# Attention's drain and the first blocks of two dense layers, recorded as one region: five weight conversions, two in-blocks and the PSUM pools put in other places

## The chip, the cores and the metric

The kernel runs on one core of a Trainium2 chip. The metric is the device time of one launch in microseconds (us). The time before is the median of three runs. Times inside the kernel come from one profiled execution, whose clock starts with the span. TensorE is PE in the rows, its weight loads PEld; VectorE is DVE, ScalarE ACT, GpSimd POOL, SyncE SP.

## The reference

Sliding-window attention with a few sink keys feeds two dense layers, one after the other; nothing but the last result is written out.

```python
# q, k, v: (2, 8, 768, 64) fp32; n_sink = 4, window = 128
keep = is_sink | ((rel >= 0) & (rel < window))
a = softmax(where(keep, q @ k.T / 8, -1e9))
x = (a @ v) as (1536, 512)              # tokens x model width
h = np.maximum(x @ w_in1, 0.0)          # w_in: (512, 2048)
x = h * h @ w_out1                      # w_out: (2048, 512)
h = x @ w_in2                           # the second layer
g = h * np.tanh(log1p(exp(h)))
out = g @ w_out2                        # (1536, 512) fp32
```

The weights come in fp64 and are read as pairs of 32-bit words; q, k and v are fp32. A product in the layers must be as exact as fp32, so each operand is held as a high and a low part (names in h and l: `xh`, `xl`, `wih`, `wil`, `woh`, `wol`, `gh`, `gl`), and each product is three matmuls, low times high, high times low, high times high.

## The kernel before, in words

**Attention.** The work is cut into 48 pairs of heads: two batches, six tiles of 128 tokens, four pairs a tile. One loop, with `n` from -3 to 52, runs all of it as a pipeline: in step n the scores of pair n+4 are made (`emit_s`, L398), the exponentials of pair n+3 (L419), the sums' reciprocals (L430, L431) and POOL's normalisation of two pairs (L439), the transposes of two pairs (L451), their copies out of PSUM (`pts`, L466) and the products with v of pairs n-4 and n-3 (L488). When the four pairs of a tile are through, ACT copies the result out of PSUM (`xf`, L503), POOL makes its high part (L504) and its low part (L506); for the last two tiles DVE makes the low part instead, two steps later (`split_x`, L513). From n = 44 on no new scores are made: this is the **drain**. It lies between some 75 and 90 us of the span.

**Layers.** The hidden width of 2048 is cut into 16 blocks of 128, the tokens into three groups of 512. For one group and one block there is an **in-block** (12 matmuls at L195, x with `wi`, into one PSUM bank `h`) and an **out-block** (12 matmuls at L658, g with `wo`, added up over the 16 blocks in four banks `o`). Between them, for layer one, ACT does relu, square and the cast to the high part `gh` (L204, L205, L206) and DVE the low part `gl` (L209). `slot(n)` emits in-block n and, one block behind in layer one (`LAG`), the out-block.

**Conversions.** The weights of a block, `wi` and `wo`, are converted in the first pass, each by one `Conv`: SP loads 512 KB of raw words (three buffers, so a load waits until the third one before it has been read), `head` on ACT (L128) or POOL (L130) scales the high words, DVE clears all but their sign (`mid_r1`, L136), writes 16 bits of the low words (`mid_r2`, L142, the 16-bit step) and joins both (`mid_or`, L148, the or-step); `high` is a cast on ACT (L167) and `low` a subtraction on DVE (L171). The heads and the or-step's operands stand in five buffers. In the layers a planner gives two conversions to each slot, in the order of `needed` and without those in `done_w`. Inside attention they are placed by hand: `PLAN` says in which step n which stages of which block run, the block numbers 0 to 3 being wi0, wo0, wi1, wo1. `PLAN` holds three of them, wi0, wo0 and wi1; in-blocks 0 and 1 are emitted in the steps `IN_AT`, so that the planner starts at the first out-block and in-block 2.

**Order.** Both parts are recorded under `tc.manual_schedule()`, attention in one region and the layers in a second: what is written first is issued first on its engine. Attention's PSUM holds four banks for scores and early in-blocks (`ps_s`), three for transposes (`ps_p`) and one for results (`ps_a`), in this order. The layers' pools take the same eight banks: `ps_h` the first four, `ps_o` the last four. A bank is handed on when its last reader is done.

Of the kernel before, what the change touches and what calls it, by code (L numbers as in the profile page):

```python
# [9 lines left out]
F32 = mybir.dt.float32  # L10
# [6 lines left out]
PSUM = bass.MemoryType.PSUM  # L17
P = 128
# [5 lines left out]
def f32(ap):  # L24
    return ap.bitcast(F32)
# [3 lines left out]
def kernel(  # L29
# [17 lines left out]
    NB = S // P  # L47
    NPAIR = H // 2
    NDC = DM // P
    TS = 512  # L50
# [133 lines left out]
    conv = main.enter_context(tc.tile_pool(name="conv", bufs=2))  # L184
    W1N = 2
    EV = (0, 2)
    w1pool = main.enter_context(tc.tile_pool(name="w1pool", bufs=1))
    gpool = main.enter_context(tc.tile_pool(name="gpool", bufs=1, reuse_waits="tile"))
    wt = {}


    def in_products(ph, w, sp):
        for m, (a, x) in enumerate([("wil", xh[sp]), ("wih", xl[sp]), ("wih", xh[sp])]):
            for d in range(NDC):
                nc.tensor.matmul(  # L195
                    ph, lhsT=w[a][:, d, :], rhs=x[:, d, :],
                    start=(m == 0 and d == 0), stop=(m == 2 and d == NDC - 1),
                )

    def new_g(pool):  # L200
        return [pool.tile([P, TS], F32R, tag=nm, name=nm, bufs=2) for nm in ("gh", "gl")]

    def relu_squared(ph, gh):
        nc.scalar.activation(out=ph, in_=ph, func=AF.Relu)  # L204
        nc.scalar.activation(out=ph, in_=ph, func=AF.Square)  # L205
        nc.scalar.copy(gh, ph)  # L206

    def low_part(x, gh, gl):
        nc.vector.tensor_tensor(out=gl, in0=x, in1=f32(gh), op=ALU.subtract)  # L209


    att = ExitStack()
    apool = att.enter_context(tc.tile_pool(name="apool", bufs=1))
    ps_s = att.enter_context(tc.tile_pool(name="ps_s", bufs=4, space=PSUM, reuse_waits="tile"))
    ps_p = att.enter_context(tc.tile_pool(name="ps_p", bufs=3, space=PSUM, reuse_waits="tile"))
    ps_a = att.enter_context(tc.tile_pool(name="ps_a", bufs=1, space=PSUM, reuse_waits="tile"))

    tiles = [(b, i) for b in range(B) for i in range(NB)]
    qn, kn, vn = {}, {}, {}
# [280 lines left out]
    def emit_x(b, i):  # L500
        hi, lo = x_slot(b, i)
        x = apool.tile([P, NPAIR, P], F32, tag="xf", name="xf", bufs=1)
        nc.scalar.copy(x, av.pop((b, i)))  # L503
        nc.gpsimd.tensor_copy(hi, x)  # L504
        if b * NB + i < len(tiles) - 2:
            nc.gpsimd.tensor_tensor(out=lo, in0=x, in1=f32(hi), op=ALU.subtract)  # L506
        else:
            st["x"] = (x, hi, lo)
# [4 lines left out]
            nc.vector.tensor_tensor(out=lo, in0=x, in1=f32(hi), op=ALU.subtract)  # L513

    blocks = []
    for fb in range(W1N):
        wt[0, fb] = weight_tiles(w1pool, fb)
        blocks += [Conv(conv, 0, fb, part, wt[0, fb]) for part in ("wi", "wo")]
    WARM = (6, 3, 2, 1)
    PLAN = {  # L520
        0: {5: "load", 11: "head", 14: "mid_r1", 18: "mid_r2", 22: "mid_or", 26: "high low"},
        2: {36: "load", 41: "head_pool", 44: "mid_r", 45: "mid_or", 46: "high low"},
        1: {37: "load", 46: "head mid_r", 47: "mid_or", 48: "high low"},
    }

    IN_AT = (46, 48)
    SINKS = {n0 + 2 * (i - 2): i for n0 in (-1, NB * NPAIR - 3) for i in range(2, NB)}
    early, ready = {}, {}
    NPR = len(pairs)
    with tc.manual_schedule():  # L530
        load_limits()
        nc.scalar.preload_act_table_set("natural_log_exp_and_others")
        load_tile(0, "qk", halves=2)
        load_tile(1, "qk")
        load_tile(2, "kq")
        load_tile(0, "v")
        load_tile(3, "kq")
        positions()
        load_tile(1, "v")
        load_tile(2, "v")  # L540
        load_rest(2)
        warm = apool.tile([P, P], F32, name="warm")
        nc.vector.memset(warm, 0.0)
        nc.vector.memset(one, 1.0)
        nc.gpsimd.memset(two, 2.0)
        for x in prs:
            nc.gpsimd.memset(x[:, :, WIN:], 0.0)
        for x in sums:
            nc.vector.memset(x, 1e-9)
        idle = ps_a.tile([P, P + 2], F32, tag="av", name="idle")  # L550

        def keep_warm(times):
            for _ in range(times):
                nc.tensor.matmul(idle[:, 0:P], lhsT=warm, rhs=warm, start=True, stop=True)  # L554

        keep_warm(WARM[0])
        limits(idle[:, P : P + 2])
        first_mask()
        prep(0, "q", 0)
        keep_warm(WARM[1])  # L560
        prep(0, "k", 0)
        keep_warm(WARM[2])
        emit_s(*pairs[0])
        emit_max(*pairs[0], 0)
        emit_max(*pairs[0], 1)
        prep(0, "q", 1)
        prep(0, "k", 1)
        emit_s(*pairs[1])
        emit_max(*pairs[1], 0)
        emit_max(*pairs[1], 1)  # L570
        second_mask()
        window_masks()
        emit_exp(*pairs[0])
        for n in range(-3, NPR + 5):
            at = {d: pairs[n + d] for d in range(-4, 5) if 0 <= n + d < NPR}
            last = {d for d in at if at[d][2] == NPAIR - 1}
            t, j = divmod(n, NPAIR)
            if n % 2 and 0 in at:
                emit_t([at[-1], at[0]])
            if 4 in at and n > -3:  # L580
                emit_s(*at[4])
            if 3 in at and n > -3:
                emit_exp(*at[3])
            if 4 in at and n > -3:
                emit_max(*at[4], 0)
            if 4 in at and n > -3:
                emit_max(*at[4], 1)
            if n % 2 == 0:
                split_x()
                group = [at[d] for d in (2, 3) if d in at]  # L590
                if group:
                    emit_rs(group)
                for p in group:
                    emit_norm(*p)
            if -4 in last:
                emit_x(*at[-4][:2])

            if n % 2 == 0:
                if n >= 0 and j == 2:
                    prep_rows(t + 2)  # L600
                for d in (-4, -3):
                    if d in at:
                        emit_av(*at[d])
            for _ in range((1, 2, 0, 1)[j]):
                evac_t()
            if n in (-3, -2):
                prep(1, "qk"[n + 3])
            if n >= 0 and j == NPAIR - 1:
                load_tile(t + 4, "q", halves=1 + (t + 5 == len(tiles)))
                load_tile(t + 4, "k", halves=1 + (t + 6 >= len(tiles)))  # L610
                load_tile(t + 3, "v")
                load_rest(t + 3)
            if n in SINKS:
                sink_keys(SINKS[n])
            if n < 0:
                keep_warm(WARM[3])
            if n == 1:
                fast_flag()
            for fb in range(W1N):
                if n == IN_AT[fb]:  # L620
                    early[fb] = ps_s.tile([P, TS], F32, tag="s", name="h")
                    in_products(early[fb], wt[0, fb], 0)
                if n == IN_AT[fb] + 1:
                    ready[fb] = new_g(gpool)
                    relu_squared(early[fb], ready[fb][0])
                if n == IN_AT[fb] + 2:
                    low_part(early[fb], *ready[fb])
            for m, steps in PLAN.items():
                for step in steps.get(n, "").split():
                    getattr(blocks[m], step)()  # L630
    att.close()


# [259 lines left out]
    w2pool = mo.enter_context(tc.tile_pool(name="w2pool", bufs=1, reuse_waits="tile"))  # L893
    ps_h = mo.enter_context(tc.tile_pool(name="ps_h", bufs=4, space=PSUM, reuse_waits="tile"))
    ps_o = mo.enter_context(tc.tile_pool(name="ps_o", bufs=4, space=PSUM, reuse_waits="tile"))
    engines = [getattr(mybir.EngineType, e) for e in ("PE", "DVE", "Activation", "Pool", "SP")]
    tc.mark_branch_hint_location("general", hint="LikelyTaken", engines=engines)
    with tc.manual_schedule():
        moe(
            wt, lambda fb: w1pool if fb < W1N else w2pool, conv, gpool, ps_h, ps_o,  # L900
            done_in=ready, done_w=[(0, blocks[m].fb, blocks[m].part) for m in PLAN],
        )
    mo.close()
    main.close()

# [97 lines left out]
    with tc.If(is_fast == 0, label="general"):  # L1003
        dense_attention()
        gm = ExitStack()
        conv = gm.enter_context(tc.tile_pool(name="conv2", bufs=2))
        wpool = gm.enter_context(tc.tile_pool(name="wpool2", bufs=1))
        tmp = gm.enter_context(tc.tile_pool(name="tmp2", bufs=1))
        ps_h = gm.enter_context(tc.tile_pool(name="ps_h2", bufs=4, space=PSUM))
        ps_o = gm.enter_context(tc.tile_pool(name="ps_o2", bufs=4, space=PSUM))  # L1010
# [36 lines left out]
```

## Time and profile before

| what | value |
|---|---|
| median of 3 runs | 614.74 us (614.39 to 615.74) |
| the profiled execution | 614.09 us |
| its span | 612.3 us |
| PE busy | 602.5 us, 98% of the span |
| PEld busy | 493.7 us, 81% |
| DVE busy | 452.9 us, 74% |
| ACT busy | 349.6 us, 57% |
| POOL busy | 70.6 us, 12% |

The span is what lies between the first and the last instruction; the execution's own time is 1.8 us longer. Busy shares are means over the whole span, and the kernel has two parts with different limits, so they say little on the place that the change touches. In the profile's picture of 40 equal slices (15.3 us each) PE stands at nine tenths or more in all but two, the sixth (76.5 to 91.8 us) and the last.

### The profile page before, as it was taken

How to read it: one execution, taken by the hardware profiler on the slowest of the kernel's cores; microseconds unless marked ns; L12 is line 12 of the kernel's file. 1: busy time of each engine (PE TensorE's matmuls, PEld its weight loads, DVE VectorE, ACT ScalarE, POOL GpSimd, SP SyncE). 2: the span in 40 equal slices, each digit the busy share in tenths (PEclk: the TensorE clock that was granted, in tenths of full speed). 3: DMA queues.
4: the chain of work that ended last, by engine and by line, in shares of the span. 5: the costliest groups of instructions: out<-in, count | busy, mean ns of one | idle time of the engine just before them, and what ended most of it. 6: DMA issues, size and time to landing. Idle time of an engine off the chain costs nothing.

```text
span 612.3 us, 10256 instructions
## 1 busy us (share of the span) xinstructions
PE 602.5 (98%) x3854; PEld 493.7 (81%) x3854; DVE 452.9 (74%) x951; ACT 349.6 (57%) x723; POOL 70.6 (12%) x103
## 2 busy tenths in 40 slices
PE   9999989999999999999999999999999999999996
PEld 6786778888888888888888888888888888888885
DVE  5898889989621111188889699999888778887784
ACT  4999976777643333277777555555454444544442
POOL 5889940000000000000000000000000000000000
PEclk9999999999999999999999999999999999999999
DMA  9989746666400000036666300000010000100001
GB/s 190 191 179 185 195 139 179 202 204 196 148 1 0 2 0 1 0 113 197 205 190 193 101 1 2 0 1 1 1 69 1 0 1 0 44 27 1 0 1 71
DMA packets 71704, 49.45 MB, mean 81 GB/s; under 512 B 49508, under 2 KB 66148, under 8 KB 71652
## 3 DMA queue, kind: packets, MB, share of 16 engines
q1 hardware_dynamic: 71360, 48.38, 29.1%
q8 instruction: 31, 0.51, 0.3%
q10 hardware_dynamic: 292, 0.39, 0.2%
q14 instruction: 21, 0.17, 0.1%
HBM read 45.61 MB, written 3.15 MB: 80 GB/s over the span
## 4 chain that ended last, share of the span: by engine, by line
PE 94%; DVE 2%; POOL 1%; ACT 1%; issue 1%; DVEq 0%; ACTq 0%; POOLq 0%
PE o L658 43%; PE h L195 42%; PE s L398 3%; PE av L488 3%; PE pt L451 2%; PE idle L554 1%; PE tr L346 1%; POOL pr L439 1%; DVE cv_r L142 0%; PE tr L328 0%; ACT pr L419 0%; DVE cv_a L148 0%; DVE pts L466 0%; DVE s L409 0%; DVE cv_r L136 0%
## 5 line engine op out<-in xcount | busy, mean ns | idle before, releaser
L195 PE MATMUL h<-xh,wil 128*128 128x512 f32 x384 | 102.9, 390 | 0.0
L195 PE MATMUL h<-xl,wih 128*128 128x512 f32 x384 | 102.6, 389 | 0.0
L195 PE MATMUL h<-xh,wih 128*128 128x512 f32 x384 | 102.6, 389 | 0.0
L209 DVE TENSOR_TENSOR gl<-h,gh 128x512 fp32r<-128x512 f32 x48 | 33.2, 691 | 89.7 <-ACT gh L206 89.7
L195 PEld LDWEIGHTS h<-xl,wih 128*128 128x128 f32 x384 | 72.1, 188 | 15.0
L195 PEld LDWEIGHTS h<-xh,wih 128*128 128x128 f32 x384 | 72.1, 188 | 15.0
L195 PEld LDWEIGHTS h<-xh,wil 128*128 128x128 f32 x384 | 71.9, 188 | 15.0
L658 PE MATMUL o<-gh,wol 128*128 128x512 f32 x192 | 74.8, 390 | 1.5 <-DVE wol L171 1.5
L726 ACT ACTIVATE e<-t,small 128x512 f32<-128x512 f32 x48 | 34.8, 725 | 70.4 <-DVE t L722 70.4
L658 PE MATMUL o<-gh,woh 128*128 128x512 f32 x192 | 74.7, 389 | 0.0
L658 PE MATMUL o<-gl,woh 128*128 128x512 f32 x192 | 74.7, 389 | 0.0
L204 ACT ACTIVATE h<-h 128x512 f32<-128x512 f32 x48 | 27.9, 582 | 77.9 <-PE h L195 77.9
L658 PE MATMUL o<-wol,gh 128*128 128x512 f32 x176 | 68.5, 389 | 0.0
L658 PE MATMUL o<-woh,gl 128*128 128x512 f32 x176 | 68.5, 389 | 0.0
L658 PE MATMUL o<-woh,gh 128*128 128x512 f32 x176 | 68.5, 389 | 0.0
L742 ACT CAST gh<-t 128x512 fp32r<-128x512 f32 x44 | 27.4, 623 | 46.4 <-PE o L658 43.0
L148 DVE SCALAR_TENSOR_TENSOR cv_a<-cv_a,cv_r 128x512 int32<-128x512 int32 x64 | 44.6, 697 | 6.2
L209 DVE TENSOR_TENSOR gl<-t,gh 128x512 fp32r<-128x512 f32 x44 | 30.3, 689 | 19.8 <-ACT gh L742 19.8
L419 ACT ACTIVATE pr<-s,nm 128x208 f32<-128x208 f32 (+2 forms) x96 | 40.5, 436 | 5.3 <-DVE nm L409 4.9
L439 POOL TENSOR_TENSOR pr<-pr,rs 128x416 f32<-128x416 f32 (+2 forms) x48 | 42.3, 902 | 9.5 <-DVE rs L431 6.3
L658 PEld LDWEIGHTS o<-gh,wol 128*128 128x128 f32 x192 | 36.0, 188 | 8.9 <-DVE wol L171 1.6
L128 ACT ACTIVATE cv_a<-raw 128x512 f32<-128x512 f32 x63 | 42.3, 673 | 0.2 <-DMA raw<-in_moe_w_in_dram 0.2
(107 smaller groups left out, 998.1 us busy)
## 6 DMA issues: line engine op xcount, KB each, us to landing
raw<-in_moe_w_in_dram SPq DMA_DIRECT2D x32, 512.0 KB, 4.0
raw<-in_moe_w_out_dram SPq DMA_DIRECT2D x32, 512.0 KB, 4.3
vn<-in_v_dram SPq DMA_DIRECT2D x12, 256.0 KB, 5.7
qn<-in_q_dram SPq DMA_DIRECT2D x10, 256.0 KB, 5.0
kn<-in_k_dram SPq DMA_DIRECT2D x9, 256.0 KB, 4.6
vx<-in_v_dram SPq DMA_DIRECT2D x16, 128.0 KB, 4.1
out_dram<-ob SPq DMA_DIRECT2D x8, 256.0 KB, 2.4
kn<-in_k_dram SPq DMA_DIRECT2D x6, 128.0 KB, 3.0
```

What stands on the lines that cost most here:

```text
L128: nc.scalar.activation(out=self.a, in_=high_words, func=AF.Copy, scale=2.0**-112)
L148: nc.vector.scalar_tensor_tensor(out=ai, in0=ai, scalar=3, in1=self.r, op0=ALU.logical_shift_left, op1=ALU.bitwise_or)
L195: nc.tensor.matmul(ph, lhsT=w[a][:, d, :], rhs=x[:, d, :], start=(m == 0 and d == 0), stop=(m == 2 and d == NDC - 1),)
L204: nc.scalar.activation(out=ph, in_=ph, func=AF.Relu)
L209: nc.vector.tensor_tensor(out=gl, in0=x, in1=f32(gh), op=ALU.subtract)
L398: nc.tensor.matmul(banks[e][qs, 0:w], lhsT=kt[r, j, q1], rhs=kt[r, j, k0 : k0 + w], start=True, stop=True, skip_group_check=True,)
L419: nc.scalar.activation(out=pr[b, i][:, 2 * j + e, 0:w], in_=banks[e][:, 0:w], func=AF.Exp, bias=nm[:, e : e + 1], scale=-1.0, accum_out=sm ...
L439: nc.gpsimd.tensor_tensor(out=x, in0=x, in1=rs.to_broadcast([P, 2, w]), op=ALU.mult)
L488: nc.tensor.matmul(av[b, i][e * D : (e + 1) * D, j, qs], lhsT=x[0:kv, 2 * j + e, :], rhs=pts[0:kv, c, e, qs], start=(j == 0 and m == 0), s ...
L658: nc.tensor.matmul(acc[sp][t], lhsT=a, rhs=x, start=(fb == 0 and m == 0), stop=(fb == NFB - 1 and m == 2),)
L726: nc.scalar.activation(out=e, in_=t, func=AF.Ln, bias=two)
L742: nc.scalar.copy(g_tiles(n)[0], et[n][1])
```

## The change

The two regions become one. The PSUM pool `ps_a` is made first, ahead of `ps_s` and `ps_p`. `PLAN` gets two more conversions, numbers 4 (wi2) and 3 (wo1), and the others' steps move; the head of number 2 (wi1) goes from POOL to ACT. In-blocks 0 and 1 are emitted in steps 44 and 49 instead of 46 and 48, and ahead of the step's other work; their relu, square and cast follow at the end of the same step, their low parts in steps 45 and 51. Of the last two attention tiles only the last but one has its low part on DVE. The weights of block 2 get buffers in the first pool, because they are now converted inside attention.

```diff
@@ PSUM pools
+    ps_a = att.enter_context(tc.tile_pool(name="ps_a", bufs=1, space=PSUM, reuse_waits="tile"))
     ps_s = att.enter_context(tc.tile_pool(name="ps_s", bufs=4, space=PSUM, reuse_waits="tile"))
     ps_p = att.enter_context(tc.tile_pool(name="ps_p", bufs=3, space=PSUM, reuse_waits="tile"))
-    ps_a = att.enter_context(tc.tile_pool(name="ps_a", bufs=1, space=PSUM, reuse_waits="tile"))
@@ emit_x
-        if b * NB + i < len(tiles) - 2:
+        if b * NB + i != len(tiles) - 2:
             nc.gpsimd.tensor_tensor(out=lo, in0=x, in1=f32(hi), op=ALU.subtract)
@@ blocks, PLAN
-    for fb in range(W1N):
+    for fb in range(W1N + 1):
...
-        2: {36: "load", 41: "head_pool", 44: "mid_r", 45: "mid_or", 46: "high low"},
-        1: {37: "load", 46: "head mid_r", 47: "mid_or", 48: "high low"},
+        2: {36: "load", 44: "head mid_r mid_or", 45: "high", 46: "low"},
+        1: {37: "load", 45: "head mid_r1", 46: "mid_r2 mid_or", 47: "high", 48: "low"},
+        4: {38: "load", 48: "head mid_r1", 49: "mid_r2 mid_or high", 50: "low"},
+        3: {46: "load", 50: "head mid_r", 51: "mid_or", 52: "high low"},
...
-    IN_AT = (46, 48)
+    IN_AT, LOW_AT = (44, 49), (45, 51)
...
-    with tc.manual_schedule():
+    order = ExitStack()
+    order.enter_context(tc.manual_schedule())
+    if True:
@@ the loop over n: at its start
+            for fb in range(W1N):
+                if n == IN_AT[fb]:
+                    early[fb] = ps_s.tile([P, TS], F32, tag="s", name="h")
+                    in_products(early[fb], wt[0, fb], 0)
@@ the loop over n: at its end
-            for fb in range(W1N):
-                if n == IN_AT[fb]:
-                    early[fb] = ps_s.tile([P, TS], F32, tag="s", name="h")
-                    in_products(early[fb], wt[0, fb], 0)
-                if n == IN_AT[fb] + 1:
-                    ready[fb] = new_g(gpool)
-                    relu_squared(early[fb], ready[fb][0])
-                if n == IN_AT[fb] + 2:
-                    low_part(early[fb], *ready[fb])
             for m, steps in PLAN.items():
                 for step in steps.get(n, "").split():
                     getattr(blocks[m], step)()
+            for fb in range(W1N):
+                if n == IN_AT[fb]:
+                    ready[fb] = new_g(gpool)
+                    relu_squared(early[fb], ready[fb][0])
+                if n == LOW_AT[fb]:
+                    low_part(early[fb], *ready[fb])
     att.close()
@@ the layers
-    with tc.manual_schedule():
-        moe(
-            wt, lambda fb: w1pool if fb < W1N else w2pool, conv, gpool, ps_h, ps_o,
-            done_in=ready, done_w=[(0, blocks[m].fb, blocks[m].part) for m in PLAN],
-        )
+    moe(
+        wt, lambda fb: w1pool if fb <= W1N else w2pool, conv, gpool, ps_h, ps_o,
+        done_in=ready, done_w=[(0, blocks[m].fb, blocks[m].part) for m in PLAN],
+    )
+    order.close()
```

What this does to the built order is seen at three places. The first is PE's queue at the beginning of the drain, just behind the last scores; `h` is in-block 0, `av` are the products with v of pairs 40 and 41.

```order
 L451 MATMUL pt<-ident,pr_108 128x64 x16
 L398 MATMUL s<-kt 64x208 x4
+L195 MATMUL h<-xh_67,wil_111 128x512 x4
+L195 MATMUL h<-xl_70,wih_110 128x512 x4
+L195 MATMUL h<-xh_67,wih_110 128x512 x4
 L488 MATMUL av<-pts,vn 64x64 x2
 L488 MATMUL av<-pts,vx 64x64 x4
```

In-block 0 stands ahead of these products now; it stood behind them, before the next transposes.

The second place is ACT's queue where in-block 1 is turned into g: numbers at the end of a name are buffers, `h_2041` and `gh_2056` before and `h_2055` and `gh_2071` now are in-block 1, and the digit behind `wih` or `woh` is the weight block. Before:

```order
L167 CAST woh0_112<-cv_a_1987 128x512
L204 ACTIVATE h_2041<-h_2041 128x512
L205 ACTIVATE h_2041<-h_2041 128x512
L206 CAST gh_2056<-h_2041 128x512
L503 COPY xf_2078<-av_2022 128x512
L167 CAST wih2_2121<-cv_a_2109 128x512
L128 ACTIVATE cv_a_2131<-raw_2107 128x512
L167 CAST woh1_116<-cv_a_2115 128x512
```

Now:

```order
L167 CAST woh0_112<-cv_a_1981 128x512
L128 ACTIVATE cv_a_2051<-raw_1740 128x512
L167 CAST wih2_118<-cv_a_2051 128x512
L204 ACTIVATE h_2055<-h_2055 128x512
L205 ACTIVATE h_2055<-h_2055 128x512
L206 CAST gh_2071<-h_2055 128x512
L128 ACTIVATE cv_a_2093<-raw_2005 128x512
L503 COPY xf_2098<-av_2032 128x512
L167 CAST woh1_116<-cv_a_2093 128x512
```

The head and the cast of wi2 stand ahead of in-block 1's three steps; the cast reads what DVE's or-step on `cv_a_2051` leaves.

The third place is DVE's queue ahead of the low part of in-block 2, the last row of both pieces. Before:

```order
L171 TENSOR_TENSOR wol1_117<-cv_a_2115,woh1_116 128x512
L136 TENSOR_SCALAR cv_r_2140<-raw_2127 128x512
L142 TENSOR_SCALAR cv_r_2140<-raw_2127 128x512
L148 SCALAR_TENSOR_TENSOR cv_a_2139<-cv_a_2139,cv_r_2140 128x512
L171 TENSOR_TENSOR wil3_2162<-cv_a_2131,wih3_2161 128x512
L136 TENSOR_SCALAR cv_r_2172<-raw_2129 128x512
L142 TENSOR_SCALAR cv_r_2172<-raw_2129 128x512
L148 SCALAR_TENSOR_TENSOR cv_a_2171<-cv_a_2171,cv_r_2172 128x512
L171 TENSOR_TENSOR wol2_2124<-cv_a_2139,woh2_2123 128x512
L209 TENSOR_TENSOR gl_2189<-h_2175,gh_2188 128x512
```

Now:

```order
L171 TENSOR_TENSOR wol2_121<-cv_a_2136,woh2_120 128x512
L136 TENSOR_SCALAR cv_r_2161<-raw_2148 128x512
L142 TENSOR_SCALAR cv_r_2161<-raw_2148 128x512
L148 SCALAR_TENSOR_TENSOR cv_a_2160<-cv_a_2160,cv_r_2161 128x512
L171 TENSOR_TENSOR wil4_2183<-cv_a_2152,wih4_2182 128x512
L136 TENSOR_SCALAR cv_r_2193<-raw_2150 128x512
L142 TENSOR_SCALAR cv_r_2193<-raw_2150 128x512
L148 SCALAR_TENSOR_TENSOR cv_a_2192<-cv_a_2192,cv_r_2193 128x512
L171 TENSOR_TENSOR wol3_2145<-cv_a_2160,woh3_2144 128x512
L209 TENSOR_TENSOR gl_2210<-h_2196,gh_2209 128x512
```

The same in-block's low part stands behind the conversions of wo2, wi4 and wo3 where it stood behind those of wo1, wi3 and wo2: each slot of the layers works two conversions further ahead.

## Rows read from the trace of the kernel before

**Rows 1.** Stretches of the span (us): busy time of each engine.

```profile
core 0: us, PE busy (x) PEld busy (x) DVE busy (x) ACT busy (x) POOL busy (x), PEclk, DMA share, GB/s
80.00:100.00 20.00, 18.42 (x147) 14.84 (x147) 18.73 (x35) 15.04 (x27) 3.91 (x5) 1.00 0.58 180
...
130.00:140.00 10.00, 10.00 (x45) 8.26 (x45) 8.91 (x18) 7.23 (x13) 0.00 (x0) 1.00 0.63 186
```

**Rows 2.** The chain in order of time, 77 to 97 us: start, length, what.

```profile
77.82 0.17 DVE rs L430
...
79.14 1.42 DVE cv_r L142
...
81.84 0.63 ACT wih L167
...
89.58 0.61 DVE wol L171
...
90.24 3.02 PE o L658 x12
93.26 2.72 PE h L195 x12
```

**Rows 3.** Timeline of PE: start, length, instruction, [idle before, who ended it].

```profile
76.43 0.34 PE L488 MATMUL av<-pts,vn 128*64 128x64 f32 x4 [0.34 <-ACT xf L503]
...
78.31 0.46 PE L451 MATMUL pt<-ident,pr 64*128 64x64 f32 x8 [0.33 <-POOL pr L439]
...
90.24 0.50 PE L658 MATMUL o<-gh,wol 128*128 128x512 f32 x1 [1.47 <-DVE wol L171]
...
101.48 0.39 PE L658 MATMUL o<-gl,woh 128*128 128x512 f32 x1
```

**Rows 4.** Timeline of DVE, 78 to 100 us.

```profile
78.68 0.42 DVE L136 TENSOR_SCALAR cv_r<-raw 128x512 int32<-128x512 int32 x1
...
81.04 0.76 DVE L148 SCALAR_TENSOR_TENSOR cv_a<-cv_a,cv_r 128x512 int32<-128x512 int32 x1
...
96.42 0.42 DVE L136 TENSOR_SCALAR cv_r<-raw 128x512 int32<-128x512 int32 x1
96.87 0.47 DVE L142 TENSOR_SCALAR cv_r<-raw 128x512 uint16<-128x512 uint32 x1
97.44 0.69 DVE L148 SCALAR_TENSOR_TENSOR cv_a<-cv_a,cv_r 128x512 int32<-128x512 int32 x1
98.05 0.68 DVE L171 TENSOR_TENSOR wol<-cv_a,woh 128x512 fp32r<-128x512 f32 x1
98.65 0.68 DVE L209 TENSOR_TENSOR gl<-h,gh 128x512 fp32r<-128x512 f32 x1
```

**Rows 5.** Timeline of ACT, 87 to 92 us.

```profile
87.72 0.58 ACT L204 ACTIVATE h<-h 128x512 f32<-128x512 f32 x1 [0.33 <-PE h L195]
88.33 0.58 ACT L205 ACTIVATE h<-h 128x512 f32<-128x512 f32 x1
88.95 0.59 ACT L206 CAST gh<-h 128x512 fp32r<-128x512 f32 x1
89.43 0.59 ACT L503 COPY xf<-av 128x512 f32<-128x512 f32 x1
89.91 0.63 ACT L167 CAST wih<-cv_a 128x512 fp32r<-128x512 f32 x1
90.43 0.69 ACT L128 ACTIVATE cv_a<-raw 128x512 f32<-128x512 f32 x1
```

**Rows 6.** Timeline of POOL, 74 to 80 us.

```profile
75.04 1.53 POOL L130 TENSOR_SCALAR cv_a<-raw 128x512 f32<-128x512 f32 x1
```

**Rows 7.** The page's DMA issues: KB each, median us from issue to landing.

```profile
raw<-in_moe_w_out_dram SPq DMA_DIRECT2D x32, 512.0 KB, 4.3
```

**Rows 8.** Stretches at the end of the span; the last matmul ends in the first.

```profile
607.00:608.00 1.00, 0.34 (x2) 0.00 (x0) 0.61 (x2) 0.37 (x1) 0.00 (x0) 1.00 0.99 377
...
610.00:611.00 1.00, 0.00 (x0) 0.00 (x0) 0.00 (x0) 0.00 (x0) 0.00 (x0) 0.74 0.03 8
611.00:612.00 1.00, 0.00 (x0) 0.00 (x0) 0.00 (x0) 0.00 (x0) 0.00 (x0) 0.50 0.00 0
```

## The prediction, made before the changed kernel ran

> **What bounds the kernel now.** I read four views in this order: stretches, the chain that ended last, then the timelines of PE, DVE and ACT over the place that the edit touches. Read the stretches [rows 1] for one thing: inside the layers PE is busy for all of every stretch (10.00 of 10 us), while the stretch from 80 to 100 us leaves PE 1.58 us idle. Once the layers run dense, PE alone sets the pace, and whatever PE loses in attention's drain or in the first blocks is carried to the end unchanged. So the question is only when PE gets through the first blocks.
>
> The chain in time [rows 2] says what holds that place. From 77.82 us to 90.24 us the chain runs almost wholly over DVE (one ACT cast between), and it ends in the wol part of block 0, which the first out-block's first matmul needs. PE's own timeline agrees [rows 3]: it waits 0.34 us for the xf copy, 0.33 us for POOL's normalisation, and 1.47 us for that wol, 2.14 us in all. Later, at 101.48, PE reads the gl of in-block 2 with no wait; DVE began that gl at 98.65 and took 0.68 [rows 4], so it was ready about 2.1 us early. Those 2.1 us are the only slack in the place. DVE is the bound of the drain, not PE and not ACT.
>
> **What the change does on each engine.** PE: in-block 0 moves ahead of the attention products of pairs 40 and 41. No matmul is added; PE is filled where it waited 0.34 and 0.33 us, so both can go: a gain of at most 0.67 us there, and PE reaches the first out-block at 90.24 - 1.47 - 0.67 = 88.10 us. POOL: it loses the head of block 2, 1.53 us [rows 6], and gets the low part of the last attention tile (it belongs to the third group of tokens, first read two groups of 16 blocks of 2 x 2.72 us later [rows 2], 174 us, so its place is free). ACT: gets that head, 0.69 us [rows 5], some 4 us ahead of the first ACT step that the chain holds (81.84) [rows 2]; cost 0. SP: one load of 512 KB moves ahead of where it stood, the others keep their order; loads are priced below.
>
> DVE: here is the term that decides. The planner in the layers is told that five conversions are done, so its slots 0, 1 and 2 now hold the next ones: wi3, wo2, wi4, wo3 and the first half of wi5, where wi2, wo1, wi3, wo2 and half of wi4 stood. In-block 2 is the same block in both kernels, and its gl stands behind all of them. DVE therefore does two whole conversions more before that gl. One conversion is four instructions, whose starts are 0.45, 0.57, 0.61 and 0.60 us apart (96.42, 96.87, 97.44, 98.05, 98.65) [rows 4]: 2.22 us. Two are 4.44 us, against 2.1 us of slack, and DVE was the bound before it: there is no idle DVE time in front into which they could go.
>
> **The sum, step by step.** DVE starts the first conversion of the drain at 78.68 in both. Its first three instructions and one pts copy are the same four instructions in another order; before, they take until 81.65 (81.04 plus 0.61) [rows 4]. I take 81.65 for the change too. Uncontended they would take 0.45 + 0.57 + 0.60 + 0.60 = 2.22 us instead of 2.97; the 0.75 us between is the 16-bit step, which took 1.42 us there [rows 2] and 0.47 at 96.87. POOL was busy beside it before, and its normalisation of the last pairs, 1.5 us earlier without the head, is still beside it now. The Trainium skill, GPSIMD Engine Reference, section Key points, says that GpSimd shares its SBUF interfaces with VectorE and contends with two-port and two-input instructions. By that rule the 1.42 us stays, by a free POOL the sum would be 0.75 us smaller.
>
> Then eleven DVE instructions follow back to back: the first mask step of wo0 0.45, gl 0, wil1 0.60 each, wo0's 16-bit step 0.57 and its or-step 0.60, xl, pts and wol0 0.60 each, and wi2's three, 0.45, 0.57, and 0.69 to its end: 87.98 us. ACT now casts wih2 only after that (88.03; 0.05 us is the hand-over, as 90.24 after 89.58 + 0.61 shows within a few hundredths). Behind the cast wait, on ACT, the three steps of in-block 1 and the head of wo1. Their starts are 0.52, 0.61, 0.62 and 0.48 us apart and the head takes 0.69 [rows 5]: ACT ends the head at 90.95. DVE meanwhile does wil2 (from 88.70, behind the cast's 0.62) and two steps of wo1, and waits at its or-step until 91.00. That step 0.60 and gl 1 0.69: 92.29 us.
>
> In the built program the first matmul of out-block 0 waits for this gl 1. Its accumulator takes the bank that in-block 1 held, since the pools now stand in another order; before, it took a bank of the transposes. PE goes on at 92.33, against 90.24: **2.09 us lost**, with 4.2 us idle.
>
> The second wait: the or-step of wo1 releases ACT's cast of woh1, and DVE takes wol1 at 92.40, 0.60 us. Then five half conversions of 1.62, four low parts of 0.60 and gl 2, 0.69: 8.10 + 2.40 + 0.69 from 93.00 gives 104.19. PE reads it at 104.24. PE alone would be there at 92.33 + 4 blocks of 2.72 + 0.23 = 103.44. So **0.80 us more**, and against 101.48 in all **2.76 us**. Every later slot holds 5.04 us of DVE work (two conversions and a gl) against PE's 5.44, so nothing is lost further on, and nothing is won back.
>
> Loads: raw takes 4.3 us from issue to landing [rows 7]. The load of wo3 is issued after the 16-bit step of wi3, at 94.0, lands at 98.3, and DVE reads it first at 99.06 (after three half conversions and two low parts): it fits, by 0.8 us. Cost taken 0; at the other end, a load 1.3 us later than the row says lets DVE's chain slip by 0.5 us.
>
> The profiled execution took 614.09 us; the sum gives 616.85. The median of the runs shown is 0.65 us above the profiled one, so the forecast for the median is 614.74 + 2.76 = **617.5 us**. About 0.2% (1.2 us) is what a measurement of this kernel can tell from no change.
>
> **The rivals.** First, **no change**: DVE runs the same list without one wait and without contention. From 78.68 the 41 instructions up to gl 2 then take 23.07 us (mine: 25.51, with 0.75 for POOL and 1.69 of three waits for ACT, 0.81, 0.67 and 0.21). That ends at 101.75, and PE is 0.32 us late: 615.1 us. It is the floor of the DVE work. For it: POOL does end earlier. Against it: the cast of wih2 stands ahead of in-block 1's steps on ACT's queue, which makes two of these waits certain. It decides if these costs are under about 0.9 us instead of 2.44. Chance 0.10.
>
> Second, **faster**: the drain's 2.14 us of PE waits [rows 3] go and no new one comes: 612.6 us. That needs gl 2 by 99.3, so DVE's list in 20.6 us, which is under the floor of 23.07. It could only come from DVE steps that run quicker than any row shows. Chance 0.04.
>
> Third, **the clock**. After the last matmul PE is idle, and the granted clock of 1.00 (the upper level, 2.4 GHz) is 0.74 between 610 and 611 and then 0.50, the lower level [rows 8], some 3 us after it stopped. The new idle stretch is 4.2 us. The Trainium skill, TensorE: Matmul & The Clock Gate, section Why this matters for your kernels, says that an idle stretch of about this kind between bursts puts the clock back, and it speaks against this change. If out-block 0 runs at half, it takes 2.72 us more; 0.80 of that passes inside the second wait, so 1.92 remains: 619.4 us. For it: the row. Against it: no row shows a fall between two bursts. How long it would stay is not shown either; from 0 to both of the next blocks (another 2.72 us) is possible. Chance 0.17.
>
> **How the numbers follow.** My forecast has 0.69, with its own bounds from 616.7 (POOL contends with nothing, less 0.75) to 618.0 (loads, plus 0.5). The range 615.8 to 619.0 holds that, the lower half of the clock's case (0.09) and the upper edge of the first rival (0.03). Faster 0.04; within 0.2% 0.09, from the first rival; slower 0.87.
>
> **What would show it.** Right: PE idle of some 4 us before the first out-block, released by DVE's gl at L209 and not by wol; a second PE wait near 104 us for gl; DVE busy without larger gaps from 78 to 104; the waits of 0.34 and 0.33 us gone; the layers after 110 us all PE. Wrong: the first out-block starts before 90.2 us, or gl 2 ends before 102 us. If the granted clock falls under 1.00 around 92 us, the third rival holds.

## The result, and the profile after

The changed kernel takes **619.66 us** (median of 6 runs, 618.88 to 620.74), the kernel before 615.04 (6 runs in the same sessions, 614.39 to 616.09): a ratio of 1.0075, with a 95% interval of 1.006 to 1.009. It is slower by 4.6 us. The forecast was 617.5 and its range ended at 619.0: the sign was right, the size was not.

The profiled execution took 619.09 us, its span is 617.3. Four of its views answer to the rows of before. The first is the chain in order of time; its last reduce of attention's sums (L430) is the mark from which places are counted below, because the profiled executions come to it at different times (77.11 to 78.53 us).

```profile
77.34 0.17 DVE rs L430
...
88.53 0.62 ACT wih L167
...
92.15 0.61 DVE gl L209
...
92.81 4.94 PE o L663 x12
97.75 2.74 PE h L195 x12
```

Before, the chain's last DVE step ahead of the first out-block was wol [rows 2]; now it is gl at L209, the low part of in-block 1. The out-block behind it takes 4.94 us there, where 12 matmuls took 3.02 before. PE's timeline says when it waited.

```profile
82.00 0.71 PE L451 MATMUL pt<-ident,pr 64*128 64x64 f32 x15 [0.41 <-DVE pts L466]
83.13 0.34 PE L488 MATMUL av<-pts,vn 128*64 128x64 f32 x4 [0.42 <-ACT xf L503]
...
88.03 0.29 PE L488 MATMUL av<-pts,vn 128*64 128x64 f32 x4
92.81 0.79 PE L663 MATMUL o<-gh,wol 128*128 128x512 f32 x1 [4.49 <-DVE gl L209]
...
105.77 0.39 PE L663 MATMUL o<-gh,wol 128*128 128x512 f32 x1
106.00 0.40 PE L663 MATMUL o<-gl,woh 128*128 128x512 f32 x1
```

The waits of 0.34, 0.33 and 1.47 us [rows 3] are gone; 0.41, 0.42 and 4.49 stand in their place. Out-block 2 starts at 105.77. From the mark that is 28.43 us, and 23.43 before (its second matmul at 101.48 [rows 3], its first at 101.25): 5.00 us later. PE reads gl 2 at 106.00 without a wait. The stretches show the granted clock, in the last column but two.

```profile
85.00:90.00 5.00, 3.31 (x42) 2.52 (x40) 4.18 (x9) 2.62 (x5) 0.00 (x0) 1.00 0.60 178
90.00:91.00 1.00, 0.00 (x0) 0.00 (x0) 0.67 (x2) 0.97 (x3) 0.00 (x0) 0.56 0.40 160
91.00:92.00 1.00, 0.00 (x0) 0.00 (x0) 0.54 (x1) 0.90 (x2) 0.04 (x1) 0.50 0.00 0
...
96.00:97.00 1.00, 1.00 (x4) 0.81 (x3) 0.97 (x3) 0.80 (x2) 0.00 (x0) 0.52 0.47 90
97.00:98.00 1.00, 1.00 (x6) 0.82 (x5) 0.90 (x3) 0.58 (x2) 0.00 (x0) 1.00 0.97 377
...
110.00:120.00 10.00, 10.00 (x46) 8.29 (x45) 9.45 (x19) 7.72 (x15) 0.00 (x0) 1.00 0.67 206
```

PE stood still from 88.32 (88.03 plus 0.29). The clock went to its lower level, 1.2 GHz, between 90 and 91 us and came back just before 97, while out-block 0 ran from 92.81 to 97.59: 4.78 us instead of 2.72, so 2.06 us lost. Behind that, PE has no idle time. The last view is DVE's timeline.

```profile
79.07 1.03 DVE L142 TENSOR_SCALAR cv_r<-raw 128x512 uint16<-128x512 uint32 x1
80.21 1.14 DVE L148 SCALAR_TENSOR_TENSOR cv_a<-cv_a,cv_r 128x512 int32<-128x512 int32 x1
...
89.19 0.69 DVE L171 TENSOR_TENSOR wil<-cv_a,wih 128x512 fp32r<-128x512 f32 x1 [0.68 <-ACT wih L167]
...
91.46 0.69 DVE L148 SCALAR_TENSOR_TENSOR cv_a<-cv_a,cv_r 128x512 int32<-128x512 int32 x1 [0.75 <-ACT cv_a L128]
92.07 0.68 DVE L209 TENSOR_TENSOR gl<-h,gh 128x512 fp32r<-128x512 f32 x1
92.83 1.70 DVE L171 TENSOR_TENSOR wol<-cv_a,woh 128x512 fp32r<-128x512 f32 x1
...
105.12 0.69 DVE L209 TENSOR_TENSOR gl<-h,gh 128x512 fp32r<-128x512 f32 x1
```

Two things are to be seen. The wol at 92.83 took 1.70 us, where every other takes 0.68 or 0.69; POOL made the low part of the last attention tile beside it, as its timeline shows:

```profile
92.70 1.29 POOL L506 TENSOR_TENSOR xl<-xf,xh 128x512 fp32r<-128x512 f32 x1
```

And gl 2, the row at 105.12, was ready at 105.81, only 0.19 us before PE read it. So **two limits end at the same place**: PE, with its wait and the low clock, and DVE, with its list up to gl 2. A trace names only the one that came last; which of them costs the time had to be tried.

### The profile page after: what moved, and what is told of

It reads as the page before. It is cut to its first block, busy times and chain, and to the rows that moved or that the text cites. A ratio compares the mean times of both kernels' runs of the same rounds, so it can differ in the third digit from the quotient of the medians.

```text
span 617.3 us, 10241 instructions
## 1 busy us (share of the span) xinstructions
PE 603.7 (98%) x3854; PEld 494.6 (80%) x3854; DVE 453.9 (74%) x950; ACT 350.4 (57%) x724; POOL 70.2 (11%) x103
## 4 chain that ended last, share of the span: by engine, by line
PE 92%; DVE 4%; ACT 1%; POOL 1%; issue 1%; DVEq 0%; ACTq 0%; POOLq 0%
PE o L663 43%; PE h L195 41%; PE s L398 3%; PE av L488 2%; PE pt L451 1%; PE idle L558 1%; PE tr L346 1%; POOL pr L439 1%; DVE s L409 1%; DVE pts L466 1%; DVE cv_a L148 1%; ACT pr L419 1%; DVE cv_r L142 1%; PE tr L328 0%; DVE cv_r L136 0%
## 5 line engine op out<-in xcount | busy, mean ns | idle before, releaser
L209 DVE TENSOR_TENSOR gl<-h,gh 128x512 fp32r<-128x512 f32 x48 | 33.1, 690 | 92.7 <-ACT gh L206 92.6
L209 DVE TENSOR_TENSOR gl<-t,gh 128x512 fp32r<-128x512 f32 x44 | 30.3, 690 | 19.5 <-ACT gh L747 19.5
```

## The experiments

All runs in one table. The last column is the start of out-block 2 from the mark (last L430) in the run's profile; where PE waits again or runs at the low clock behind that place, the time is later than the column says. The ratio is to the kernel before, measured in the same session: 615.04 for the changed kernel, 614.36 to 614.38 for all rows below it. Between sessions the ratios are the safer comparison.

| run | median us (runs) | ratio, 95% interval | out-block 2 |
|---|---|---|---|
| before | 615.04 (6) | | 23.43 |
| changed | 619.66 (6) | 1.0075, 1.006 to 1.009 | 28.43 |
| changed, bank apart | 621.17 (5) | 1.0111, 1.0095 to 1.0127 | 27.39 |
| changed, slots later | 619.74 (6) | 1.0079, 1.0064 to 1.0093 | 29.02 |
| changed, both | 615.06 (12) | 1.0010, 1.0001 to 1.0020 | 24.04 |
| changed, PE kept busy | 619.45 (6) | 1.0075, 1.0060 to 1.0089 | 27.40 |
| both, low part on DVE | 614.43 (11) | 1.0000, 0.9991 to 1.0009 | 23.59 |
| and order of need | 613.59 (11) | 0.9989, 0.9980 to 0.9997 | 22.30 |
| and two copies to ACT | **612.19** (7) | 0.9968, 0.9956 to 0.9979 | 21.72 |
| before, two copies to ACT | 613.76 (11) | 0.9994, 0.9985 to 1.0003 | 22.90 |
| before, one region | 618.55 (6) | 1.0067, 1.0055 to 1.0079 | 28.65 |
| best, slots undone | 618.37 (4) | 1.0069, 1.0054 to 1.0083 | 25.08 |
| best, bank undone | 618.16 (4) | 1.0059, 1.0044 to 1.0074 | 27.60 |

**Which of the two limits.** Four kernels answer this. The first takes the bank away from the wait:

```diff
                 if n == IN_AT[fb]:
+                    if fb == 1:
+                        skip = ps_s.tile([P, TS], F32, tag="s", name="skip")
+                        nc.tensor.matmul(skip[:, 0:P], lhsT=warm, rhs=warm, start=True, stop=True)
                     early[fb] = ps_s.tile([P, TS], F32, tag="s", name="h")
```

> One bank of the scores' pool is taken (and touched by one small matmul) ahead of in-block 1, so that out-block 0's first accumulator no longer shares in-block 1's bank. Theory A (two limits end at the same place: PE's wait with the low clock, and DVE's list up to the gl of in-block 2, which ended at 105.81 in the changed kernel where PE read it at 106.00): out-block 0 starts at about 88.4 us instead of 92.81, yet the first matmuls of out-block 2 still come at 105.8; PE then waits there some 4 us instead, and if the clock falls in that wait as it did in the other, about 2 us more are lost after it: 619.5 us without the fall, 621.5 with it; not faster in either case. Rival B (the wait of 4.49 us and the clock after it are the loss): 615.0 us.

Measured: 621.17 us, 1.5 us above the changed kernel (ratios of 1.0111 and 1.0075, whose intervals do not overlap). The largest wait of the trace is gone, and nothing is won. PE's timeline has the wait at out-block 2 now, and the stretches (two lines, clock in the last column but two) have the fall of the clock behind it.

```profile
105.14 0.72 PE L666 MATMUL o<-gh,wol 128*128 128x512 f32 x1 [3.23 <-ACT gh L206]
106.20 0.80 PE L666 MATMUL o<-gl,woh 128*128 128x512 f32 x1 [0.34 <-DVE gl L209]
```

```profile
104.00:106.00 2.00, 0.72 (x1) 0.22 (x1) 1.90 (x4) 1.97 (x4) 0.00 (x0) 0.81 0.92 273
106.00:108.00 2.00, 1.80 (x4) 1.49 (x5) 1.86 (x5) 0.93 (x3) 0.00 (x0) 0.50 0.51 182
```

The second, where the conversions come one slot later:

```diff
-            conv_at[m // 2 - (0 if done_w else AHEAD)].append(key)
+            conv_at[m // 2 + (1 if done_w else -AHEAD)].append(key)
```

> The planner's conversions come one slot later, as many ahead of in-block 2's gl as in the kernel before; bank and wait stay as changed. Theory A: gl 2 is ready at about 101.4, but PE comes there only at 105.8 after its wait and the low clock: no change, 619.6 us (within 0.4). Rival C (DVE's two conversions more are the whole loss, PE's wait is covered): 4.4 us faster, 615.2 us.

Measured: 619.74, no change. DVE now stands idle ahead of gl 2 and waits for PE's in-block by way of ACT:

```profile
103.64 0.69 DVE L209 TENSOR_TENSOR gl<-h,gh 128x512 fp32r<-128x512 f32 x1 [2.35 <-ACT gh L206]
```

The third has both edits.

> Both edits of the two runs before together. Theory A: out-block 0 at 88.4, in-block 2 at 91.95 (its bank waits for the xf copy), out-block 1 at 94.7, in-block 3 at 98.45 (wil3), out-block 2 at 101.2: as the kernel before, 615.1 us (614.7 to 615.7), no fall of the clock. Rivals B and C: 615 us too, but each of them would have it from one edit alone.

Measured: 615.06, the time of the kernel before within 0.2% (the interval, 1.0001 to 1.0020, leaves it slower by some 0.1%). Each edit alone gave nothing, both together gave 4.0 us by the ratios and 4.6 by the medians: the limits were in parallel. PE's two longest waits in the first blocks are small, and the clock is 1.00 in every stretch of them:

```profile
92.50 1.20 PE L195 MATMUL h<-xh,wil 128*128 128x512 f32 x4 [0.47 <-ACT xf L503]
...
99.04 1.21 PE L195 MATMUL h<-xh,wil 128*128 128x512 f32 x4 [0.74 <-DVE wil L171]
```

The fourth takes away the clock's part alone:

```diff
+            if n == NPR + 4:
+                busy = ps_s.tile([P, TS], F32, tag="s", name="busy")
+                for _ in range(18):
+                    nc.tensor.matmul(
+                        busy, lhsT=wt[0, 0]["wih"][:, 0, :], rhs=xh[0][:, 0, :], start=True, stop=True
+                    )
     att.close()
```

> The changed kernel with 18 matmuls more of 512 columns on a free bank, between attention's last product and out-block 0, 0.23 us each, 4.1 us together, where PE waited; nothing reads their result. They keep PE busy, so the granted clock should stay at 1.00 and out-block 0 take 2.72 us and not 4.78. Theory A: PE is then at out-block 2 by 103.7, and waits until 105.86 for gl 2: no change, 619.5 us; up to 621.5 if the clock falls in the new wait. Rival B: 617.6 us, the 2.06 us of the low clock come back in full.

Measured: 619.45, no change, with the clock at 1.00 from 86 to 112 us; in the changed kernel its two halves from 90 to 92 us stood at 0.56 and 0.50:

```profile
90.00:92.00 2.00, 2.00 (x11) 1.64 (x10) 1.22 (x3) 1.94 (x5) 0.00 (x0) 1.00 0.43 172
```

PE comes to out-block 2 earlier by 1.77 us from the mark (105.28 - 0.74 - 77.88 = 26.66, against 28.43) and waits there, first for ACT and then for DVE:

```profile
93.35 0.50 PE L669 MATMUL o<-gh,wol 128*128 128x512 f32 x1 [0.16 <-DVE gl L209]
...
105.28 0.51 PE L669 MATMUL o<-gh,wol 128*128 128x512 f32 x1 [0.74 <-ACT gh L206]
...
106.36 0.50 PE L669 MATMUL o<-gl,woh 128*128 128x512 f32 x1 [0.57 <-DVE gl L209]
```

From the mark (77.88 in this profile) gl 2 is read at 28.48 us, and in the changed kernel at 106.00 - 77.34 = 28.66. The low clock is real, and in the changed kernel it costs 0.2 us by these two profiles, less than the times can tell. So theory A holds, and rivals B and C fall.

A third queue runs close beside the two. In the changed kernel gl 2 starts some 0.08 us after DVE is through with its list, because ACT's gh is late, and ACT's steps up to gh follow without a gap on a head that waited for its load:

```profile
102.18 0.68 ACT L128 ACTIVATE cv_a<-raw 128x512 f32<-128x512 f32 x1 [1.49 <-DMA raw<-in_moe_w_in_dram]
```

In the first and the fourth kernel that wait is 0.66 and 0.81 us, and DVE goes from the wol of block 1 to gl 2 without a gap. So there the list, and not the loads, is the second limit.

**POOL beside DVE.** The next run starts from the kernel with both edits and takes the low part of the last tile off POOL:

```diff
-        if b * NB + i != len(tiles) - 2:
+        if b * NB + i < len(tiles) - 2:
...
-                split_x()
+                if n < NPR + 4:
+                    split_x()
...
+            if n == NPR + 4:
+                split_x()
     att.close()
```

> The kernel with the bank and the slots undone (615.06 us), and in addition the low part of the last attention tile back on DVE, as in the kernel before, placed behind attention's last step. In that kernel DVE's wol of block 1 took 1.71 us (93.39 to 95.10) while POOL made that low part, against 0.68 for every other wol. Theory: POOL's work slows DVE's; then wol 1 takes 0.68 again, DVE does 0.60 more itself, and wil3, for which PE waited 0.74, comes 0.4 us earlier: 614.7 us. Rival: the 1.71 has another cause, DVE has 0.60 us more to do: 615.6 us.

Measured: 614.43. In the kernel without this edit DVE's wol of block 1 took 1.71 us:

```profile
93.39 1.71 DVE L171 TENSOR_TENSOR wol<-cv_a,woh 128x512 fp32r<-128x512 f32 x1
```

With it, it has its usual length:

```profile
94.04 0.69 DVE L171 TENSOR_TENSOR wol<-cv_a,woh 128x512 fp32r<-128x512 f32 x1
```

PE's wait for wil3 went from 0.74 to 0.38 us, as forecast. The price of POOL's instruction on DVE is shown, 1.02 us; in the time the gain of 0.6 is at the edge of what these runs can tell, as the two intervals overlap.

**Is DVE's list really the pace?** If so, a list in the order of need must beat the kernel before. The next run places the steps so:

```diff
-        2: {36: "load", 44: "head mid_r mid_or", 45: "high", 46: "low"},
-        1: {37: "load", 45: "head mid_r1", 46: "mid_r2 mid_or", 47: "high", 48: "low"},
-        4: {38: "load", 48: "head mid_r1", 49: "mid_r2 mid_or high", 50: "low"},
-        3: {46: "load", 50: "head mid_r", 51: "mid_or", 52: "high low"},
+        2: {36: "load", 44: "head mid_r mid_or", 46: "high low"},
+        1: {37: "load", 47: "head mid_r mid_or", 48: "high", 49: "low"},
+        4: {38: "load", 48: "head mid_r", 49: "mid_or", 51: "high", 52: "low"},
+        3: {46: "load", 49: "head", 50: "mid_r mid_or", 51: "high", 52: "low"},
...
-    IN_AT, LOW_AT = (44, 49), (45, 51)
+    IN_AT, LOW_AT = (44, 49), (45, 52)
```

> The same, with the steps placed anew in the order in which PE needs them: ACT's head of wo1 and in-block 1's relu, square and cast and the xf copy ahead of the cast of wih2, the cast of wih1 ahead of the head of wo0, low parts behind the steps that cover their casts. The two DVE waits (0.69 for the cast of wih2, 0.74 for the head of wo1) and PE's wait for xf (0.47) should go. Theory (DVE's list and its waits set the pace of the first blocks): out-block 2 at about 99.6 us against 102.1 with bank and slots undone: 612.8 us, faster than the kernel before by 1.6. Rival: the waits only move to DMA or to ACT: 614.7.

Measured: 613.59, faster than the kernel before (0.9980 to 0.9997), but by 0.8 us and not 1.6: the waits went, as PE's timeline shows with a single one left from 74 to 130 us, and the size was too high.

```profile
82.33 0.71 PE L451 MATMUL pt<-ident,pr 64*128 64x64 f32 x15 [0.44 <-DVE pts L466]
```

That last one is for a copy of transposes on DVE. The next run moves it:

```diff
-        copy = nc.vector.tensor_copy if r and pair_no[group[0]] % 4 in EV else nc.scalar.copy
+        copy = nc.vector.tensor_copy if r and pair_no[group[0]] % 4 in EV and pair_no[group[0]] < NPR - 4 else nc.scalar.copy
```

> The same, and DVE's two last copies of transposes (0.60 us each) go to ACT, which waits 1.53 and 2.25 us there. Theory: DVE's list before the first blocks is 1.2 us shorter, out-block 2 at about 98.6 us: 611.9 us. Rival (DVE no longer bounds, PE or ACT do): as the run before it, 612.8 us.

Measured: **612.19 us**, 0.9956 to 0.9979 of the kernel before: the best version, faster than the kernel before and than the run without this edit. It lies 0.3 us from the theory's 611.9, and the rival, no gain over the run without this edit, falls. Out-block 2 starts 1.71 us earlier than before, counted from the mark. What is left is one wait of 0.53, for the xf copy on ACT. DVE's gl 2 at 99.00 (ready 99.68) is read by the second matmul of the out-block that starts at 99.75:

```profile
83.23 0.34 PE L488 MATMUL av<-pts,vn 128*64 128x64 f32 x4 [0.53 <-ACT xf L503]
...
99.75 0.39 PE L669 MATMUL o<-gh,wol 128*128 128x512 f32 x1
```

The same edit alone, on the kernel before:

> The kernel before with that one edit alone: its two last DVE copies of transposes go to ACT. Theory (DVE bounds the drain): wol 0, for which PE waited 1.47 us, comes up to 1.2 us earlier, and gl 2 too: 613.3 us. Rival (ACT's queue becomes the bound there, its casts come 0.5 us later each): 614.4 us, no change.

Measured: 613.76, 0.9985 to 1.0003: between the two, so inconclusive in the time. The trace agrees with the theory in part: PE's wait for wol 0 is 0.86 instead of 1.47 us [rows 3], 0.6 shorter and not 1.2. The rest of the theory failed: gl 2 ends 21.59 us after the mark, and 21.51 before, so it came no earlier. Part of what DVE gained it spent on a wait of 0.47 for POOL's xh, ahead of the last tile's low part.

```profile
88.96 0.50 PE L658 MATMUL o<-gh,wol 128*128 128x512 f32 x1 [0.86 <-DVE wol L171]
```

**The region alone.** The kernel before, with its two regions made one and nothing else:

```diff
-    with tc.manual_schedule():
+    order = ExitStack()
+    order.enter_context(tc.manual_schedule())
+    if True:
         load_limits()
...
-    with tc.manual_schedule():
+    if True:
         moe(
...
+    order.close()
     mo.close()
```

> The kernel before with the two regions made one, and nothing else changed. Its built order differs on ACT and DVE alone: in two regions the first work of the layers (the heads and the first three DVE steps of wi2 and wo1) stands among the last steps of attention; in one region it stands behind them. Theory (DVE's list decides, and its gap while in-block 1 is made is now empty): out-block 0 no longer waits (1.47 us less), but wil2 ends at about 95.2 instead of 92.0, PE waits some 3 us there, and out-block 2 comes at about 103.3 against 101.25: 616.4 us, up to 618.4 if the clock falls in that wait. Rival (wol 0 was the wait that counted, it goes): 612.9 us.

Measured: 618.55 us, 1.0055 to 1.0079. PE's wait for wil2 and, in the stretch around it, the fall of the clock:

```profile
94.90 2.07 PE L195 MATMUL h<-xh,wil 128*128 128x512 f32 x4 [2.93 <-DVE wil L171]
```

```profile
94.00:96.00 2.00, 1.10 (x3) 0.91 (x4) 1.86 (x5) 1.31 (x2) 0.00 (x0) 0.54 0.60 177
```

DVE's timeline shows why wil2 is late:

```profile
89.13 0.69 DVE L209 TENSOR_TENSOR gl<-h,gh 128x512 fp32r<-128x512 f32 x1 [2.12 <-ACT gh L206]
```

DVE is idle for 2.12 us ahead of gl 1, where the kernel before did the first three steps of wi2 (87.28 to 88.90). So two regions were worth 4.2 us here: what the layers record first was issued among attention's last steps, and one region ends that. The two conversions that the change adds by hand, wi2 and wo1, are those whose first steps stood there by themselves before.

**Both edits, taken back one at a time in the best version.**

> The best version so far (612.19 us) with the planner's conversions one slot earlier again, as the change has them. Theory: gl 2 stands behind two conversions more, 4.44 us of DVE, and comes at about 104.1 against 99.7; PE waits some 4.3 us for it, and the clock falls in the wait: 616.5 us without the fall, 618.5 with it. Rival (with the steps in the order of need DVE has room): 612.2 us.

> The best version so far (612.19 us) with in-block 1 again in the bank that out-block 0 takes first. Theory: out-block 0 waits for gl 1, until about 92.4 instead of 88.8, and as gl 2 is ready by 99.7 nothing hides it: 3.6 us more, 615.8 us, and 617.8 if the clock falls as it did in the changed kernel. Rival (this wait is hidden behind DVE's list also here): 612.2 us.

Measured: 618.37 and 618.16 us. Both theories hold with the fall of the clock (618.5 and 617.8), and both rivals fall. Here nothing covers either limit, and each costs its full price, some 6 us with the clock. With the slots undone PE waits twice at out-block 2, and with the bank undone at out-block 0:

```profile
102.67 0.49 PE L669 MATMUL o<-gh,wol 128*128 128x512 f32 x1 [3.18 <-ACT gh L206]
103.73 0.79 PE L669 MATMUL o<-gl,woh 128*128 128x512 f32 x1 [0.57 <-DVE gl L209]
```

```profile
91.85 0.79 PE L666 MATMUL o<-gh,wol 128*128 128x512 f32 x1 [3.76 <-DVE gl L209]
```

## Why the prediction was right in its places and wrong in its size

The two paths to out-block 2 were forecast as they are: DVE's list up to gl 2, and PE behind its wait for gl 1. But each path had a term that the sum put at nothing and that was not nothing: POOL's low part beside DVE's list, and the clock in PE's path.

- **PE reaches the first out-block at 88.10.** It was 88.32, in a profile whose mark lies 0.48 us earlier. The two waits of 0.34 and 0.33 were said to go; they went, and two others of 0.41 and 0.42 came, for a DVE copy and for xf.
- **Out-block 0 waits for gl 1, until 92.33.** Right in mechanism and nearly in size: 92.81, a wait of 4.49 against 4.2. Of the three waits of DVE for ACT the first two were forecast at 0.81 and 0.67 and measured at 0.68 and 0.75. The contention with POOL stayed, as taken, and was larger: the drain's first four DVE steps took 3.66 us (78.21 to 81.87), not 2.97, and the next eleven 0.30 more than forecast. As the start was 0.47 earlier, gl 1 ended 0.46 later, at 92.75.
- **POOL gets the low part of the last tile, its place is free.** On DVE's path this is the step that failed. It was costed at nothing, for the place in time of its reader; what stands beside it on DVE was not asked. It lay on the wol of block 1, which took 1.70 us instead of 0.68. The forecast had the steps behind that wol start at 93.00, and they started at 94.46: 0.43 from the later gl 1 and 1.03 from POOL. The trace of before held the case already. Its 16-bit step of 1.42 us at 79.14 [rows 2] was put down to POOL's normalisation, but up to 80.24 it was POOL's low part of an earlier tile that ran beside it:

```profile
78.90 1.34 POOL L506 TENSOR_TENSOR xl<-xf,xh 128x512 fp32r<-128x512 f32 x1
80.19 2.35 POOL L439 TENSOR_TENSOR pr<-pr,rs 128x416 f32<-128x416 f32 x2
```

- **gl 2 at 104.19.** Measured 105.81, 1.62 later: the 1.46 just named and 0.16 in the eleven us behind, 0.08 of them from the head that waited for its load. The loads had been priced by the DVE step that reads them, and ACT's head reads them sooner. With 1.62 more, the sum for the profiled execution is 616.85 + 1.62 = 618.5, and 619.1 for the median, just past the range's end. Another 0.5 us of the profiled execution lies behind the last matmul, where the output is written (the span is 5.0 longer, the last matmul starts at 611.48 against 606.95).
- **The clock, as a rival at 0.17 and at nothing in the sum.** On PE's path this is the term that failed. PE alone was forecast at 103.44; the later gl 1 adds 0.48 and the low clock 2.06, which makes 105.98, and PE read gl 2 at 106.00 where 104.24 was forecast. By that path alone the median would be 617.5 + 1.76 = 619.3. The argument against the rival ("no row shows a fall between two bursts") was no evidence: the kernel before never stops PE for so long. That the rival's 619.4 is nearly the measured time is in part luck: it took 2.72 for out-block 0 where 2.06 was lost, and gl 1 0.48 too early.
- **Which of the two made the miss.** Either alone is enough. With the clock held at 1.00 the kernel took 619.45; with two conversions taken from DVE's list, which is more than POOL's 1.03, it took 619.74. PE's path and DVE's end 0.2 us apart. No run takes POOL's low part alone out of the changed kernel; as an estimate from the sums above, that would have gained nothing there.
- **The rivals "no change" and "faster"** needed DVE's list without its waits; none went away.
- What was not asked at all: what **one region** does by itself. The forecast compared built orders, so its term (two conversions more ahead of gl 2) was right. That one region alone ends the weave of the layers' first steps with attention's last ones, and costs 4.2 us in the kernel before, was found only by the run of that edit.

## What to carry to other kernels

Where a large wait is seen, ask what is ready next and how long after: here the largest wait could be removed, and the low clock too, without any gain, since a second limit ended 0.2 us earlier; what the change had cost was seen only when both were taken away together. When pools are made in another order, look up which bank each first tile gets and who used it last. Work that is moved to an idle engine is not free if it slows what stands beside it in the list that sets the pace: here POOL's low part saved DVE 0.60 us and cost it 1.02.

## What the runs showed of the hardware

A DVE subtraction of two SBUF inputs that started just behind a POOL subtraction of the same kind was held up for nearly all of it: POOL's xl ran from 92.70 to 93.99, DVE's wol from 92.83 to 94.53, 0.54 after POOL's end. It took 1.70 to 1.72 us in all five kernels that have the two side by side, and 0.69 in the run without POOL's xl. The Trainium skill, SBUF — State Buffer, section Who interferes with whom, says that a DVE instruction with two SBUF inputs contends with a GpSimd instruction that reads SBUF, and that this contention is an exclusive lock on a shared pair of ports, with the order of issue deciding who blocks. The trace agrees: if DVE had waited for all of POOL's instruction, the wol would have ended at 93.99 + 0.68 = 94.67, and it ended at 94.53.

The clock fell in all six kernels in which a long wait of PE stood in the first blocks (4.49, 3.23, 4.42, 2.93, 3.18 and 3.76 us), and stayed at 1.00 there in the others, the kernel before with its 1.47 us among them. The Trainium skill, TensorE: Matmul & The Clock Gate, section Why this matters for your kernels, says that idle gaps between bursts of matmuls bring the clock down; these runs agree. The price was 2.06 us of out-block 0 in the changed kernel, and next to nothing in its time (619.66, and 619.45 with the clock held), since gl 2 was late as well.
